# A fused attention, gated convolution, Fourier and FFN kernel: how its first pair of heads is loaded and where its early weights are decoded

## The chip, the cores and the metric

The kernel runs on one core of one Trainium2 chip. The core has TensorE for matmuls (PE in the profile; its weight loads are PEld), VectorE (DVE), ScalarE (ACT), GpSimd (POOL) and SyncE, whose queue (SPq) issues nearly all DMAs. The metric is device time of one execution in microseconds (us).

## The reference

Inputs are float32. Attention over 8 batches, 8 heads, 576 positions and 64 columns a head is followed by a gated causal convolution, a two-dimensional Fourier mixing, a layer norm and a feed-forward block:

```
scores = q @ k.T / 8            # masked: a block of 64 rows sees its own and earlier blocks
attn = softmax(scores) @ v      # heads joined: x is (8, 576, 512)
gate = sigmoid(causal_conv5(x, conv_w));  x = (gate * (x @ w_val)) @ w_out
u = x + real(fft(fft(x, axis=1), axis=2))
un = (u - mean(u)) / sqrt(var(u) + 1e-6)
out = u + relu(un @ w_ch1) @ w_ch2
```

The weights w_val, conv_w, w_out, w_ch1 and w_ch2 are float64 in memory. The kernel reads their bits and makes float32 of them.

## The kernel before

The first half of the kernel, phase1, does attention, the gated convolution and the Fourier part; the second, phase2, the norm and the feed-forward block for nine groups of 512 tokens. Every float32 operand of a matmul is split into a high and a low part in a reduced format (fp32r), and a product is two or three matmuls of parts.

**Pairs and units.** Two heads form a pair; there are 32 pairs, four to a batch. A pair is nine units: units 0 to 7 are a block of 128 queries of one of its two heads, unit 8 is the last 64 queries of both. One loop runs over the unit number n (288 units and a few to drain). A unit's stages lie apart in the loop: the scores on PE (emit_qk, L417 and L418, for unit 8 L181 to L183, tile sc), the row maximum on DVE (emit_max, L441 and L449, tile mx), the exponential on ACT (emit_exp, L463, tile PB), six units later the transposes on PE (emit_t, L577, tile pt) with copies on ACT (L583, tiles PTa, PTb, PTc), and the product with v (emit_near and emit_av, L544 and L605, tile av). The first five pairs scale by the sums of the exponentials through a transpose (L513, L524, L531).

**Operands of a pair.** `load` fetches q and k of a pair as one tile each of 128 partitions (two heads of 64), `split` writes the high and low parts (QHL and KP on ACT, the low part of q on DVE, KL on POOL), and DMAs from SBUF to SBUF copy them into the places that the matmuls read: K (L375, k with one head in both halves), QD (L364) and QQ (`spread`, L388 and L390).

**Dense work.** When the four pairs of a batch are done, `dense(b)` makes the batch's convolution gate, product with w_val (tile psv), product with the folded w_out (psx) and the Fourier products (psy, pss). It is a generator; each step emits a piece. A credit decides how many steps a unit takes: 0.9 up to unit 60 (RATE0, N0), 1.25 after (RATE).

**Early weights.** `prep_weights` is a generator too. Part by part (four of w_val, four of w_out, 128 rows of 512 each) it loads raw bits into the tile XA, decodes them (`decode`: one ACT instruction L71, four DVE instructions L75, L76, L80, L82) and writes high and low parts (wv_h L55 on DVE, wv_l L274 on POOL; for w_out the fold L295 to L299 on POOL, then we_h and we_l). Then it loads the DFT tables in ten pieces through XA and casts each to its place (L321 on ACT). It advances with the steps of the loop:

```
if pend[0] is prep:
    ...
else:
    next(pend[0])
    next(prep, None)
```

So the first parts of the weights come with the first units, and the rest comes only together with the dense steps of batch 0, which start at unit 42; what is then left is run at once ahead of that batch's product with w_out.

The tile framework turns the program into one queue of instructions for each engine. Each engine works its queue strictly in order and waits on semaphores. The framework moves instructions in the queues by its own schedule, so their order is not that of the text.

Of the kernel before, what the change touches and what calls it, by code (L numbers as in the profile page):

```python
# [8 lines left out]
F32 = mybir.dt.float32  # L9
F32R = mybir.dt.float32r  # L10
# [7 lines left out]
def kernel(  # L18
# [15 lines left out]
    D = 512  # L34
# [82 lines left out]
    def phase1():  # L117
        with ExitStack() as c1:
# [44 lines left out]
            dft_t = pool.tile([P, dft.shape[1]], F32R, name="dft")  # L163
            o = [0]

            def table(n, w):
                t = dft_t[:, o[0]:o[0] + n * w]
                o[0] += n * w
                return t.rearrange("p (n w) -> p n w", w=w) if n > 1 else t
            CDH, CDL, SDH, SDL = table(2, 258), table(2, 258), table(2, 256), table(2, 256)  # L170
            CMH, CML, SMH, SML = table(2, N2), table(2, N2), table(2, N2), table(2, N2)
            CQ, CT1, CT2, ST = table(1, 258), table(1, N2), table(1, N2), table(1, N2)
# [55 lines left out]
            YD = 2  # L228
# [6 lines left out]
            def prep_weights():  # L235
                for t in (XSP, YC2, YS2):
                    nc.gpsimd.memset(t.bitcast(F32), 0.0)
                xa = XA.rearrange("p a b c -> p (a b c)")
                raws = [(xa[:, D * 2 * i:D * 2 * i + D * 2], []) for i in range(2)]
                vals = [(t[:, 0:D], []) for t in gvs]  # L240
                uP = xa[:, 4 * D:5 * D]
                cnt = [0, 0]

                def take(pool, at):
                    t, users = pool[cnt[at] % len(pool)]
                    cnt[at] += 1
                    for c in users:
                        c.run()
                    users.clear()
                    return t, users  # L250

                def load_decode(src, n, dst, more=()):
                    raw, users = take(raws, 0)
                    r = raw.bitcast(I32)[:, 0:2 * n]
                    nc.sync.dma_start(out=r, in_=src)
                    c = Chain(wait, wait, wait, *decode(r, dst), *more)
                    users.append(c)
                    return c

                def run_all(cs):  # L260
                    for c in cs:
                        c.run()

                c0 = load_decode(conv_w.bitcast(I32), 20, uP[:, 0:20], (
                    lambda: nc.vector.tensor_copy(out=cw.rearrange("p c t -> p (c t)"), in_=uP[:, 0:20]),))
                yield
                for c in range(4):
                    d, users = take(vals, 1)

                    def w_hi(d=d, h_=wv_h[:, c, :]):  # L270
                        copy(5, h_, d)

                    def w_lo(d=d, h_=wv_h[:, c, :], l_=wv_l[:, c, :]):
                        nc.gpsimd.tensor_tensor(out=l_, in0=d, in1=h_.bitcast(F32), op=ALU.subtract)  # L274
                    users.append(load_decode(w_val[c * P:(c + 1) * P, :].bitcast(I32), D, d, (w_hi, w_lo)))
                    for _ in range(YD):
                        yield
                c0.run()
                run_all([c for _, us in raws + vals for c in us])
                for t in GF:  # L280
                    nc.gpsimd.memset(t, 0.0)

                raws[:] = [(xa[:, 0:2 * D], [])]
                vals[:] = [(xa[:, 2 * D:3 * D], [])]
                yield 1
                prev = None
                for c in range(4):
                    w, users = take(vals, 1)
                    part = load_decode(w_out[c * P:(c + 1) * P, :].bitcast(I32), D, w)
                    for _ in range(YD):  # L290
                        yield

                    def fold(w=w, part=part):
                        part.run()
# [6 lines left out]
                    def e_hi(c=c):  # L301
                        copy(6, we_h[:, c, :], uP[:, 0:D])

                    def e_lo(c=c):
                        nc.gpsimd.tensor_tensor(out=we_l[:, c, :], in0=uP[:, 0:D], in1=we_h[:, c, :].bitcast(F32),
                                                op=ALU.subtract)
                    if prev is not None:
                        prev.run()
                    prev = Chain(wait, wait, wait, wait, fold, e_hi, e_lo)
                    users.append(prev)  # L310
                    yield
                prev.run()

                w = dft.shape[1] // NCH
                chunks = []
                for z in range(NCH):
                    t = xa[:, z % 4 * w:z % 4 * w + w]
                    if z > 3:
                        chunks[z - 4].run()
                    nc.sync.dma_start(out=t, in_=dft[:, z * w:z * w + w])  # L320
                    chunks.append(Chain(wait, wait, wait, lambda t=t, z=z: (  # L321
                        nc.scalar.copy if CE >> z & 1 else nc.vector.tensor_copy)(out=dft_t[:, z * w:z * w + w], in_=t)))
                    yield
                run_all(chunks)
# [15 lines left out]
            def load_v(p):  # L340
                if p >= NPAIR:
# [4 lines left out]
                    out=VV[p], in_=v[b, :, hp * P:(hp + 1) * P].rearrange("(t p) c -> p t c", p=P))  # L346

# [301 lines left out]
            def dense(b):  # L649
# [57 lines left out]
                else:  # L707
                    for _ in prep:
                        tick(list(live))
# [205 lines left out]
            N0 = 60  # L915
            RATE0 = 0.9
# [11 lines left out]
            PS = 6  # L928
            prep = prep_weights()
            prepared = [0]  # L930
            load(0)
            nc.gpsimd.memset(PB[8][:, S:640], 0.0)
            for t in QD + [QQ[h][g][rs[1 - h], 1, :] for h in range(2) for g in range(2)]:
                nc.gpsimd.memset(t.bitcast(F32), 0.0)
            split(0).run()
            spread(0, 0)
            spread(0, 1)
            load_v(0)
            load(1)
            pend = [prep]  # L940
            next(prep)
            credit = 0.0

            def step(k=1):
                while k > 0 and pend:
                    try:
                        if pend[0] is prep:
                            if prepared[0] == PS:
                                pend.pop(0)
                                continue  # L950
# [363 lines left out]
```

## Time and profile before

| | us |
|---|---|
| median of 3 runs | 1477.8 |
| lowest and highest of them | 1476.51, 1479.29 |
| the profiled execution, its time | 1476.05 |
| the profiled execution, its span (first to last instruction) | 1474.2 |

The span is cut into stretches below by the first score matmul of a pair: pair 0 begins at 11.94 us, pair 1 at 30.39, pair 2 at 50.24, pair 3 at 70.43, pair 4 at 84.75, pair 5 at 99.89, pair 6 at 118.52, pair 7 at 143.07, pair 8 at 161.92, pair 12 at 237.09. PE's busy share is over the whole stretch; "PEclk" is the TensorE clock granted, as a share of full speed (2.4 GHz; half is 1.2 GHz).

### The profile page before, as it was taken

To read this page: it belongs to the slowest core of one execution; us is meant where nothing else is said; L and a number is where in the kernel's file an instruction comes from. 1 tells how busy PE (TensorE), PEld (TensorE's weight loads), DVE (VectorE), ACT (ScalarE), POOL (GpSimd) and SP (SyncE) were. 2 spreads that over 40 slices of the span, in tenths; PEclk is the share of its full clock that TensorE was granted. 3 is DMA by queue.
4 is the path that set the end of the run, shared out by engine and by line. 5 is a ranking of instruction groups with operands and counts; after the bars stand their busy time and mean duration, and the time that the engine had idled before them with its cause. 6 is when DMAs were issued, how large, how long until landed. Compare 5 with 4: busy or idle time off the path is not lost.

```text
span 1474.2 us, 22875 instructions
## 1 busy us (share of the span) xinstructions
PE 1420.3 (96%) x8543; PEld 1205.5 (82%) x8543; DVE 815.5 (55%) x1618; ACT 644.5 (44%) x1627; POOL 309.7 (21%) x254
## 2 busy tenths in 40 slices
PE   5798999999999999999999999999999999999998
PEld 3576888999989898888788888888888888888887
DVE  5777797979797979898983222322232223222212
ACT  5687777777777777734532112121121212112110
POOL 3423232323232323222011011111011111011100
PEclk9799999999999999999999999999999999999999
DMA  7567565656565656353500010100101010010000
GB/s 207 151 161 212 152 179 145 173 148 176 146 177 147 174 150 167 99 175 114 204 29 29 0 57 1 57 0 17 42 0 57 1 53 5 0 58 1 29 0 29
DMA packets 121611, 137.22 MB, mean 93 GB/s; under 512 B 23567, under 2 KB 91421, under 8 KB 121501
## 3 DMA queue, kind: packets, MB, share of 16 engines
q1 hardware_dynamic: 120960, 135.63, 32.2%
q8 instruction: 67, 1.10, 0.3%
q14 instruction: 44, 0.35, 0.1%
q10 hardware_dynamic: 540, 0.14, 0.0%
HBM read 70.57 MB, written 19.01 MB: 61 GB/s over the span
## 4 chain that ended last, share of the span: by engine, by line
PE 73%; DVE 10%; issue 6%; DMA 4%; POOL 3%; ACT 3%; SPq 1%; DVEq 0%; ACTq 0%; POOLq 0%
PE psh L1187 8%; PE psh L1185 8%; PE psh L1186 8%; PE o L1206 8%; PE o L1204 8%; PE o L1205 8%; PE av L605 4%; PE pt L577 4%; DVE gate L632 2%; PE sc L417 2%; POOL XA L838 2%; PE sc L418 2%; PE psx L181 1%; DVE mx L449 1%; PE psx L182 1%
## 5 line engine op out<-in xcount | busy, mean ns | idle before, releaser
L1191 DVE SCALAR_TENSOR_TENSOR hl<-psh,hh 128x512 fp32r<-128x512 f32 x144 | 99.4, 690 | 398.4 <-ACT hh L1190 398.3
L1190 ACT ACTIVATE hh<-psh 128x512 fp32r<-128x512 f32 x144 | 86.1, 598 | 500.2 <-PE psh L1187 500.0
L1187 PE MATMUL psh<-UTH,W 128*128 128x512 f32 x504 | 196.2, 389 | 1.2 <-DVE W L1093 1.2
L1185 PE MATMUL psh<-UTH,W 128*128 128x512 f32 x504 | 196.2, 389 | 1.1 <-ACT W L1092 1.1
L1206 PE MATMUL o<-hl,W 128*128 128x512 f32 x504 | 196.2, 390 | 0.0
L1186 PE MATMUL psh<-UTL,W 128*128 128x512 f32 x504 | 196.1, 389 | 0.0
L1204 PE MATMUL o<-hh,W 128*128 128x512 f32 x504 | 196.1, 389 | 0.0
L1205 PE MATMUL o<-hh,W 128*128 128x512 f32 x504 | 196.0, 389 | 0.0
L463 ACT ACTIVATE PB<-sc,mx 128x128 f32<-128x128 f32 (+4 forms) x320 | 167.0, 527 | 52.8 <-DVE mx L449 29.5
L577 PE MATMUL pt<-ident,PB 128*128 128x128 f32 x800 | 141.9, 283 | 15.4 <-ACT PTb L583 8.1
L577 PEld LDWEIGHTS pt<-ident,PB 128*128 128x128 f32 x800 | 101.0, 144 | 32.5 <-ACT PTb L583 14.5
L632 DVE SCALAR_TENSOR_TENSOR gate<-XF,cw,gate 128x575 f32<-128x575 f32 (+3 forms) x128 | 122.2, 955 | 4.5 <-ACT gate L63 3.6
L1187 PEld LDWEIGHTS psh<-UTH,W 128*128 128x128 f32 x504 | 94.6, 188 | 21.3 <-DVE W L1093 1.6
L1215 POOL TENSOR_TENSOR U<-o,U 128x512 f32<-128x512 f32 x32 | 40.3, 1288 | 341.0 <-DVE o L1213 341.0
L1185 PEld LDWEIGHTS psh<-UTH,W 128*128 128x128 f32 x504 | 94.6, 188 | 21.1 <-ACT W L1092 1.5
L1206 PEld LDWEIGHTS o<-hl,W 128*128 128x128 f32 x504 | 94.5, 188 | 20.6 <-DVE hl L1191 1.0
L1204 PEld LDWEIGHTS o<-hh,W 128*128 128x128 f32 x504 | 94.6, 188 | 19.9 <-ACT hh L1190 0.2
L1205 PEld LDWEIGHTS o<-hh,W 128*128 128x128 f32 x504 | 94.6, 188 | 19.8
L1186 PEld LDWEIGHTS psh<-UTL,W 128*128 128x128 f32 x504 | 94.6, 188 | 19.6
L449 DVE TENSOR_REDUCE mx<-sc 128x1 f32<-128x384 f32 (+2 forms) x192 | 104.3, 560 | 4.4 <-PE sc L183 2.7
L417 PE MATMUL sc<-K,QQ 128*128 128x256 f32 (+2 forms) x256 | 87.9, 354 | 13.4 <-DMA QQ<-QHL 12.5
L628 POOL TENSOR_TENSOR XL<-XF,XH 128x576 fp32r<-128x576 f32 x32 | 45.9, 1434 | 249.3 <-ACT XH L57 249.1
(226 smaller groups left out, 3122.0 us busy)
## 6 DMA issues: line engine op xcount, KB each, us to landing
K<-KP SPq DMA_DIRECT2D x128, 144.0 KB, 2.5
QQ<-QHL SPq DMA_DIRECT2D x128, 128.0 KB, 2.5
rw<-in_w_ch SPq DMA_DIRECT2D x28, 512.0 KB, 7.2
VV<-in_v SPq DMA_DIRECT2D x32, 320.0 KB, 3.6
qraw<-in_q SPq DMA_DIRECT2D x32, 288.0 KB, 3.3
kraw<-in_k SPq DMA_DIRECT2D x32, 288.0 KB, 3.3
out<-U SPq DMA_DIRECT2D x36, 256.0 KB, 2.0
QQ<-QHL SPq DMA_DIRECT2D x128, 64.0 KB, 2.4
```

Source lines behind the costliest of these rows:

```text
L417: nc.tensor.matmul(t[:, o:o + w], q[:, 0, m], KK[p][h][:, 0:w], start=True, stop=False)
L449: nc.vector.reduce_max(out=mx[:, j:j + 1], in_=t, axis=AX.X, negate=one)
L463: nc.scalar.activation(out=PB[i][:, k0:k0 + w], in_=t, func=AF.Exp, bias=nm, accum_out=su[:, at + j:at + j + 1])
L577: nc.tensor.transpose(ps[:, j, :], PB[i][:, (j0 + j) * P:(j0 + j + 1) * P], ident)
L632: nc.vector.scalar_tensor_tensor(out=gate[c][:, s:S], in0=XF[:, 0:S - s], scalar=cw[:, c, 4 - s:5 - s], in1=gate[c][:, s:S], op0=ALU.mult, ...
L1185: nc.tensor.matmul(ps, W1H[f][:, c * P:c * P + P], UTH[g][:, c, :], start=(c == 0), stop=False)
L1186: nc.tensor.matmul(ps, W1H[f][:, c * P:c * P + P], UTL[g][:, c, :], start=False, stop=False)
L1187: nc.tensor.matmul(ps, W1L[f][:, c * P:c * P + P], UTH[g][:, c, :], start=False, stop=(c == 3))
L1191: nc.vector.scalar_tensor_tensor(out=l, in0=ps, scalar=0.0, in1=h.bitcast(F32), op0=ALU.max, op1=ALU.subtract)
L1204: nc.tensor.matmul(po[t], W2H[e][:, c], h, start=(e == 0), stop=False)
L1205: nc.tensor.matmul(po[t], W2L[e][:, c], h, start=False, stop=False)
L1206: nc.tensor.matmul(po[t], W2H[e][:, c], l, start=False, stop=(e == NF - 1))
```

## The change

Three things are changed.

1. **First pair.** `first_pair` takes the place of `load(0)`, `split(0)` and both `spread(0, .)`. q and k of pair 0 are loaded twice each, head by head into both halves of the partitions, in two column halves: 16 DMAs of 64 partitions, eight issued from SyncE and eight from ScalarE. They land in tiles that are free at that time (gate). ACT and DVE then write QQ, K, KL, KP and QD in place, and the 14 DMAs from SBUF to SBUF of pair 0 are gone. Its parts are emitted in the loop at units 1, 2 and 4.
2. **Early weights.** The raw bits have four places of their own in the space of the DFT tables (tile stage), which are made only after the last decode. Loads, decodes and table pieces have fixed units (VU, OU, TU) instead of coming with the steps: w_val at units 0 to 9, w_out at 13 to 25, tables at 32 to 44.
3. **Dense steps.** The credit is 1.25 from the start.

```diff
+            VU = (0, 3, 6, 9)
+            OU = (13, 17, 21, 25)
+            TU = (32, 32, 33, 33, 34, 38, 38, 39, 39, 40)
...
+                slots = [stage[:, 2 * D * i:2 * D * i + 2 * D] for i in range(4)]
...
+                load_conv()
+                load_part(w_val, 0)
+                for c in range(1, 4):
+                    at_unit(c - 1, load_part, w_val, c)
+                at_unit(0, do_conv)
+                for c in range(4):
+                    at_unit(VU[c], do_val, c)
+                    at_unit(VU[c] + 6, load_part, w_out, c)
+                    at_unit(OU[c], do_out, c)
                 for z in range(NCH):
...
+                    at_unit(TU[z], load_table, z)
+                    at_unit(TU[z] + 4, do_table, z)
...
+            def first_pair():
+
+                *KK[0], KP[0], KL[0] = k_places()
+                Q0, K0, T0 = gate[0:2], gate[2:4], XFS
+                halves = slice(0, 256), slice(256, S)
+                dma = [nc.sync.dma_start, nc.scalar.dma_start]
+                for c in halves:
+                    for x, to in ((q, Q0), (k, K0)):
+                        for h in range(2):
+                            for r in rs:
+                                dma[h](out=to[h][r, c], in_=x[0, 0][rs[h], c])
...
+                def q_part(g):
+                    c = slice(256 * g, 256 * g + 256)
+                    for h in range(2):
+                        a, z = rs[h], rs[1 - h]
+                        nc.scalar.activation(out=T0[h][z, c].bitcast(F32R), in_=Q0[h][z, c], func=AF.Copy, scale=0.125)
+                        nc.scalar.activation(out=QQ[h][g][a], in_=Q0[h][a, c].unsqueeze(1).to_broadcast([64, 2, 256]),
+                                             func=AF.Copy, scale=0.125)
+                        nc.vector.scalar_tensor_tensor(out=QQ[h][g][z, 0, :], in0=Q0[h][z, c], scalar=0.125,
+                                                       in1=T0[h][z, c], op0=ALU.mult, op1=ALU.subtract)
+
+                def k_part(c):
+                    for h in range(2):
+                        nc.vector.tensor_copy(out=KK[0][h][:, c], in_=K0[h][:, c])
+                    for h in range(2):
+                        a = rs[h]
+                        nc.vector.tensor_tensor(out=KL[0][a, c], in0=K0[h][a, c], in1=KK[0][h][a, c].bitcast(F32),
+                                                op=ALU.subtract)
...
+                q_part(0)
+                k_part(halves[0])
+                return lambda: k_part(halves[1]), lambda: q_part(1), last_part
...
-            N0 = 60
-            RATE0 = 0.9
             RATE = 1.25
...
-            load(0)
...
-            split(0).run()
-            spread(0, 0)
-            spread(0, 1)
...
-                            next(pend[0])
-                            next(prep, None)
+                        next(pend[0])
...
-                credit += RATE if n > N0 else RATE0
+                prep_at(n)
+                credit += RATE
```

The queues show what moves. The first place is the start of ACT's queue. Before, it holds (after the load of the activation table) the high parts of q and k of pair 0, a decode and the first exponential:

```order
L356 ACT_TABLE_LOAD
L356 ACTIVATE QHL<-qraw 128x576 [waits DMAHW0_49]
L57 CAST KP<-kraw 128x576 [waits DMAHW1_49]
L71 ACTIVATE XA<-XA 128x20 [waits DMAHW3_49]
L71 ACTIVATE gv_153<-XA 128x512 [waits DMAHW4_49]
L463 ACTIVATE PB_121,su<-sc,mx 128x128 [waits DVE_49,PE_49]
```

In the changed kernel it begins with eight DMA issues; DMAHW0 to DMAHW7 are the semaphores of DMAs, which all DMAs of the core take in turn:

```order
L366 DMA gate_150<-in_q 64x256 x2
L366 DMA gate_152<-in_k 64x256 x2
L366 DMA gate_150<-in_q 64x320 [waits DMAHW0_49]
L366 DMA gate_150<-in_q 64x320 [waits DMAHW2_49]
L366 DMA gate_152<-in_k 64x320 [waits DMAHW4_49]
L366 DMA gate_152<-in_k 64x320 [waits DMAHW6_49]
L374 ACT_TABLE_LOAD
L374 ACTIVATE XF_134<-gate_149 64x256 [waits DMAHW3_49]
L375 ACTIVATE QQ_117<-gate_149 64x512 [waits DMAHW1_49]
L374 ACTIVATE XF_135<-gate_150 64x256
L375 ACTIVATE QQ_119<-gate_150 64x512
L374 ACTIVATE XF_134<-gate_149 64x256 [waits DMAHW3_49]
```

The last four of the eight issues stand behind waits on the first loads, and the table load and all of ACT's work stand behind these.

The second place is PE's queue at the change from pair 0 to pair 1. Before, the transposes of units 5 to 8 of pair 0 (PB_126 to PB_129) stand ahead of the first scores of pair 1 (K_227):

```order
L524 MATMUL rt<-ident,XF_134 128x128 x2
L544 MATMUL av<-PTa_130,VV 64x256
L544 MATMUL av<-PTa_130,VV 64x128 x2
L577 MATMUL pt<-ident,PB_126 128x128 x3
L577 MATMUL pt<-ident,PB_127 128x128 x4
L577 MATMUL pt<-ident,PB_128 128x128 x4
L577 MATMUL pt<-ident,PB_129 128x128 x5
L544 MATMUL av<-PTb,VV 64x320
L417 MATMUL sc<-K_227,QQ_117 128x256
```

In the changed kernel the eight score matmuls of pair 1 (K_238, K_239) stand ahead of them:

```order
L190 MATMUL sc<-KP,QD_115 128x320
L190 MATMUL sc<-KP,QD_115 128x256
L596 MATMUL av<-PTa_130,VV 64x128
L469 MATMUL sc<-K_238,QQ_117 128x256
L470 MATMUL sc<-KL,QQ_117 128x256
L469 MATMUL sc<-K_238,QQ_117 128x256
L470 MATMUL sc<-KL,QQ_117 128x256
L469 MATMUL sc<-K_239,QQ_119 128x256
L470 MATMUL sc<-KL,QQ_119 128x256
L469 MATMUL sc<-K_239,QQ_119 128x256
L470 MATMUL sc<-KL,QQ_119 128x256
L576 MATMUL rt<-ident,XF_134 128x128 x2
```

The third place is DVE's queue in the middle of pair 0. Before, the maxima of the later units (L449) come first and one decode follows (w_val's second part, gv_154):

```order
L359 SCALAR_TENSOR_TENSOR QHL<-qraw,QHL 128x576
L447 MEMSET sc 64x64
L505 RECIPROCAL re<-su 128x2x2
L449 TENSOR_REDUCE mx<-sc 128x1 x3
L75 TENSOR_SCALAR gv_154<-gv_154 128x512
L451 TENSOR_REDUCE mx<-mx 128x1
L76 TENSOR_SCALAR gv_154<-gv_154 128x512
```

In the changed kernel two decodes, w_val's first and second part, stand ahead of the maxima of units 5 and 6 (the last row):

```order
L80 SCALAR_TENSOR_TENSOR XA<-stage,XA 128x512
L76 TENSOR_SCALAR XA<-XA 128x512
L82 SCALAR_TENSOR_TENSOR XA<-stage,XA 128x512
L80 SCALAR_TENSOR_TENSOR XA<-stage,XA 128x512
L276 CAST wv_h<-XA 128x512
L82 SCALAR_TENSOR_TENSOR XA<-stage,XA 128x512
L394 SCALAR_TENSOR_TENSOR QD_115<-gate_149,QD_115 64x64
L394 SCALAR_TENSOR_TENSOR QD_115<-gate_150,QD_115 64x64
L276 CAST wv_h<-XA 128x512
L499 MEMSET sc 64x64 x2
L501 TENSOR_REDUCE mx<-sc 128x1 x2
```

The decodes have moved ahead of scores that wait for their maxima.

## Rows read from the trace of the kernel before

**Rows 1.** The page: the span, and each engine's busy time and share.

```profile
span 1474.2 us, 22875 instructions
PE 1420.3 (96%) x8543; PEld 1205.5 (82%) x8543; DVE 815.5 (55%) x1618; ACT 644.5 (44%) x1627; POOL 309.7 (21%) x254
```

**Rows 2.** Stretches cut at pairs: length, busy of PE, PEld, DVE, ACT, POOL; clock; DMA.

```profile
0.00:11.94 11.94, 0.00 (x0) 0.00 (x1) 5.13 (x10) 3.52 (x5) 5.12 (x18) 1.00 0.75 203
11.94:30.39 18.45, 15.37 (x60) 10.53 (x60) 9.48 (x31) 11.00 (x34) 5.17 (x6) 0.81 0.76 209
30.39:50.24 19.85, 14.53 (x76) 10.47 (x76) 15.99 (x35) 11.63 (x32) 6.16 (x5) 0.77 0.59 154
50.24:70.43 20.19, 14.82 (x83) 10.26 (x82) 16.75 (x36) 13.96 (x41) 11.07 (x14) 0.84 0.54 146
70.43:84.75 14.32, 13.08 (x89) 9.83 (x88) 9.62 (x29) 11.95 (x36) 3.53 (x4) 0.95 0.54 140
84.75:99.89 15.14, 15.08 (x100) 10.35 (x99) 9.32 (x28) 12.39 (x37) 4.18 (x4) 1.00 0.72 188
99.89:118.52 18.63, 17.13 (x130) 15.02 (x128) 16.02 (x45) 14.26 (x40) 6.82 (x8) 1.00 0.71 191
118.52:143.07 24.55, 20.17 (x147) 15.81 (x146) 18.15 (x44) 19.18 (x53) 5.80 (x6) 0.93 0.72 211
143.07:161.92 18.85, 17.89 (x146) 15.71 (x144) 13.13 (x30) 15.16 (x45) 6.92 (x7) 1.00 0.57 136
161.92:237.09 75.17, 73.13 (x627) 65.60 (x625) 62.01 (x140) 56.01 (x161) 23.31 (x17) 1.00 0.64 175
```

**Rows 3.** The timeline of all engines, first 15 us: start, length, engine, line, operation, wait.

```profile
0.73 1.28 ACT L356 ACT_TABLE_LOAD   x1 [0.73 <-PEq L1301]
...
0.74 0.39 SPq L336 DMA_DIRECT2D qraw<-in_q  x1
...
3.61 0.69 ACT L356 ACTIVATE QHL<-qraw 128x576 fp32r<-128x576 f32 x1 [1.59 <-DMA qraw<-in_q]
...
4.32 0.76 DVE L359 SCALAR_TENSOR_TENSOR QHL<-qraw,QHL 128x576 fp32r<-128x576 f32 x1 [4.32 <-ACT QHL L356]
...
5.22 2.83 SPq L375 DMA_DIRECT2D K<-KP  x4
...
11.94 0.58 PE L417 MATMUL sc<-K,QQ 128*128 128x256 f32 x1 [11.94 <-DMA QQ<-QHL]
...
13.99 0.42 DVE L441 TENSOR_REDUCE mx<-sc 128x2 f32<-128x256 f32 x1
```

**Rows 4.** The chain of waits, 95 to 146 us: start, length, what.

```profile
98.74 8.00 DMA XA<-in_w_out
...
139.21 3.01 DMA XA<-in_dft
```

**Rows 5.** DVE's timeline in pair 0.

```profile
11.98 0.43 DVE L55 CAST wv_h<-gv 128x512 fp32r<-128x512 f32 x1
...
26.11 0.42 DVE L549 TENSOR_TENSOR XF<-av,XF 128x256 f32<-128x256 f32 x1 [2.20 <-PE av L544]
```

**Rows 6.** DVE's timeline in pair 1: first, last instruction of a decode, its cast.

```profile
33.03 0.43 DVE L75 TENSOR_SCALAR gv<-gv 128x512 f32<-128x512 f32 x1 [0.27 <-ACT gv L71]
...
34.68 0.69 DVE L82 SCALAR_TENSOR_TENSOR gv<-XA,gv 128x512 int32<-128x512 int32 x1
...
35.40 1.51 DVE L55 CAST wv_h<-gv 128x512 fp32r<-128x512 f32 x1
```

**Rows 7.** Waits from 11.94 to 84.75 us: who for whom, total, times, longest.

```profile
DVE sc L440 <- PE sc L418: 9.8, 5, 4.7
```

**Rows 8.** PE's timeline: two neighbouring matmuls of dense work at full clock.

```profile
82.29 0.29 PE L182 MATMUL psv<-XL,wv_h 128*128 128x288 f32 x1
82.42 0.29 PE L183 MATMUL psv<-XH,wv_l 128*128 128x288 f32 x1
```

**Rows 9.** POOL's timeline in pair 1, beside that cast.

```profile
34.89 1.74 POOL L370 TENSOR_TENSOR KL<-kraw,KP 128x576 fp32r<-128x576 f32 x1 [8.60 <-ACT KP L57]
```

More of the change, by code (lines that the diff above doesn't have):

```diff
@@ L233, in phase1, with prepare @@
             CE = 1023
-            def prep_weights():
+            def prepare():
                 for t in (XSP, YC2, YS2):
                     nc.gpsimd.memset(t.bitcast(F32), 0.0)
[L238 to L279, printed above, removed]
@@ L280, in prep_weights @@
                 for t in GF:
                     nc.gpsimd.memset(t, 0.0)
[L283 to L294, printed above, removed]
+                xa = XA.rearrange("p a b c -> p (a b c)")
@@ new lines, in prepare, with ordered @@
+                slots = [stage[:, 2 * D * i:2 * D * i + 2 * D] for i in range(4)]
+                small = stage[:, 8 * D:8 * D + 40]
+                vals = [xa[:, D * i:D * i + D] for i in range(2)]
+                uPs = [xa[:, 2 * D + D * i:2 * D + D * i + D] for i in range(2)]
+                taps = xa[:, 4 * D:4 * D + 20]
+                order = []
+                def ordered(*stages):
+                    c = Chain(*stages)
+                    order.append(c)
+                    return c
@@ L324, in prep_weights, with load_table @@
-                run_all(chunks)
+                    ordered(*decode(slots[c], w), fold, wait, wait, wait, lambda: nc.scalar.copy(out=h_, in_=uP), wait,
+                            lambda: nc.gpsimd.tensor_tensor(out=l_, in0=uP, in1=h_.bitcast(F32), op=ALU.subtract))
+                NS_, CW = 5, dft.shape[1] // NCH
+                def load_table(z):
+                    if z == 0:
+                        for o in order:
+                            o.run()
+                        make_tables()
+                    nc.sync.dma_start(out=xa[:, z % NS_ * CW:z % NS_ * CW + CW], in_=dft[:, z * CW:z * CW + CW])
@@ new lines, in do_table, with at_unit @@
+                def do_table(z):
+                    to, t = tables["dft"][:, z * CW:z * CW + CW], xa[:, z % NS_ * CW:z % NS_ * CW + CW]
+                    ordered(lambda: (nc.scalar.copy if CE >> z & 1 else nc.vector.tensor_copy)(out=to, in_=t))
+                todo = {}
+                def at_unit(n, f, *a):
+                    todo.setdefault(n, []).append((f, a))
+                load_conv()
+                load_part(w_val, 0)
+                for c in range(1, 4):
+                    at_unit(c - 1, load_part, w_val, c)
@@ L327, in phase1 @@
+                return at, rest
             NPAIR = B * NP
@@ L707, in dense @@
                 else:
-                    for _ in prep:
-                        tick(list(live))
+                    prep_rest()
+                CDH, CDL, SDH, SDL, CMH, CML, SMH, SML, CQ, CT1, CT2, ST = (
+                    tables[t] for t in "CDH CDL SDH SDL CMH CML SMH SML CQ CT1 CT2 ST".split())
                 xt = ((2, 1), (3, 1), (0, 0), (1, 0), (2, 0), (0, 1), (1, 1), (3, 0))
@@ L976, in phase1 @@
                     emit_qk(n)
+                    if n in (1, 2, 4):
+                        later[(1, 2, 4).index(n)]()
                     if i in (4, 8):
```

99 lines of the change are left out of this document (54 added, 45 removed).

## The prediction

> **What bounds the kernel now.** I read the page first: PE is busy for 96% of a span of 1474.2 us [rows 1], so a change that adds and removes no matmul can only win back time that PE loses. Where it loses is read from the table of stretches, cut at the pairs of heads [rows 2]. From pair 8 to pair 12 PE is busy 73.13 of 75.17 us at full clock: there the kernel is bound by PE. Before pair 8 it is not. Pairs 0 to 3 take 18.45, 19.85, 20.19 and 14.32 us although they hold almost no dense work, and the granted clock is 0.81, 0.77, 0.84 and 0.95 (a mix of the levels 1.2 and 2.4 GHz) in stretches where PE waits. Ahead of them lie 11.94 us without a matmul. Pair 6 takes 24.55 us, more than any later one. The timeline of the first 15 us [rows 3] shows why PE starts late: q is issued at 0.74 us, ACT has it at 3.61, four copies of k take SyncE 2.83 us, more copies follow in that queue, and the first score waits until 11.94. DVE takes its first maximum at 13.99. In the chain of waits around pairs 5 to 7 [rows 4] a load of w_out takes 8.00 us and a table piece 3.01 us: the early weights are late for batch 0's dense work.
>
> After pair 27 the queues of both programs hold the same dense columns at each pair, and the total is the same (592,762, counted over the order). So the end moves by what PE loses less before pair 8, and by nothing else. I sum in three parts.
>
> **The start.** The first loads go out at 0.74 us as before. An issue took 0.39 us and data were there 2.87 us after it (0.74 to 3.61) [rows 3], so the fourth load of each queue is issued at about 1.9 us and lands at 4.8. ACT's eighth issue waits for that and ends near 5.2; the table load of 1.28 us [rows 3], which ran beside the loads before, now follows it, to 6.5. Four ACT instructions for the first half at 0.4 to 0.65 us (from 0.69 for 576 columns [rows 3]) end at 8.6, so the first score comes at 7.6 to 8 instead of 11.94. But the first maximum gains less. ACT's queue has pair 1's q and k ahead of pair 0's first exponential, and SyncE issues their loads only behind its own eight and v: they land near 10.5. DVE has the second halves and pair 1's low part of q ahead of its first maximum. I put it at 12.5, a gain of 1.5. If a load of 64 partitions costs as much to issue as a copy of k (2.83 / 4 = 0.71 us [rows 3]), all comes 1 us later.
>
> The Trainium skill speaks against this part: "SBUF — State Buffer", section "Can I just issue two DMAs to hit both halves?", says that DMAs on two halves of the partitions serialize and that several issuing engines do not help. By that rule the second loading of the same bytes costs what it saves, and the start gains nothing; this is the first rival below.
>
> **DVE from there to pair 4.** Pair 4's first score is at 84.75 us. Up to there DVE was busy 5.13 + 9.48 + 15.99 + 16.75 + 9.62 = 56.97 us and idle 27.78 [rows 2]; 8.3 us of that idle time lie before the first maximum (13.99 less 5.13 and some 0.6 of work after 11.94 [rows 2, 3, 5]), 19.5 behind it: 7.5 in pair 0 and 3.86 + 3.44 + 4.70 = 12.0 in pairs 1 to 3.
>
> - A decode takes 33.03 to 35.37, 2.35 us [rows 6]. Six of the eight lay before pair 4 and now all eight do: + 4.7.
> - Pair 0's split is now 14 DVE instructions: 4 casts at 0.26 (half of 0.43 for 512 columns [rows 5], with some fixed cost), 8 subtractions at 0.44 (0.42 for 256 columns [rows 5]), two small ones at 0.15. That is 4.9, less the 0.76 of the old low part of q [rows 3]: + 4.1.
>
> This gives 65.8 us of work, and 7.3 us idle before the first maximum (12.5 less some 5.2 of work). What is open is the idle time behind it. If none is left, pair 4's first score comes at 73.1 (- 11.7); if all 19.5 stay, at 92.6 (+ 7.9). In pair 0 the queue of DVE now holds three and a half decodes, so nearly all of the 7.5 goes. In pairs 0 to 3 DVE waited 9.8 us for scores of PE at the first maximum of a pair [rows 7], and pair 1's scores now stand ahead of sixteen transposes; but two decodes ahead of the maxima of units 5 and 6 hold up their exponentials. I take 8.0 us, nearer to pairs 1 to 3 alone (12.0) than to nothing: 65.8 + 7.3 + 8.0 = 81.1, or **- 3.7 us**. POOL and SyncE do the same kinds of work as before here; SyncE has 14 copies fewer.
>
> **Pairs 4 to 7.** Counted over the order, pairs 8 to 11 hold 73,344 dense columns and take 75.17 us [rows 2]. A dense matmul of 288 columns takes 0.13 us from start to start [rows 8]. Pairs 4 to 7 held 50,866 columns, 22,478 fewer, or 78 matmuls, 10.1 us: at PE's pace 65.1 us. They took 77.17 (15.14 + 18.63 + 24.55 + 18.85 [rows 2]), so 12.1 were lost, and of these 9.1 in pair 6 (10,992 columns: 15.5 at PE's pace against 24.55). Now two decodes, their folds and the wait for the loads are gone from pairs 5 to 7; the ten table casts move from pairs 6 and 7 to 4 and 5, beside ACT's 12.39 of 15.14 us there. I leave 5 us of loss (0 to 12.1). With RATE 1.25 the four pairs hold 56,928 columns, so 75.17 - 7.4 + 5 = 72.8: **- 4.4 us**. The 6,062 columns more that are then done (21 matmuls, 2.7 us) and 576 more ahead of pair 4 (0.3) need not be done later: **- 3.0 us**.
>
> **The sum** is - 3.7 - 4.4 - 3.0 = - 11.1 us on the profiled execution's 1476.05: 1465.0. The median of the runs shown lies 1.75 above that execution, so I say 1466.5 for a median.
>
> **A cost that the order hides.** A cast of 512 columns took 0.43 us, and 1.51 us where a subtraction of POOL ran beside it from 34.89 to 36.63 [rows 5, 6, 9]. The Trainium skill's page "SBUF — State Buffer", section "Who interferes with whom", says that such an operation and GpSimd lock each other out of a shared port; the trace agrees with 1.51 against 0.43. The 56.97 us include such losses for the POOL work of six parts; the two folds that now also fall before pair 4 bring six more long POOL instructions. At 1.08 us each that is 6.5 at most and 0 at least; I took 0, since pair 4's queue has room for the last of them, and the second rival takes all.
>
> **Rivals.**
>
> 1. *The double load brings nothing* (0.12). The 16 loads land when the copies did, and the first maximum stays at 13.99. For it: DMA share 0.75 in the first stretch [rows 2] and the waits in ACT's queue. Against it: 14 copies leave. It costs the 1.5 us of the start: 1466.5, median 1468.
> 2. *The early decodes hold up the pairs* (0.12, slower). DVE waits as before (+ 7.9) and POOL's six instructions each lengthen one of DVE's by 1.08 us (+ 6.5). That is + 14.4 at pair 4 and + 7.0 with the rest: 1483.1, median 1485. For it: DVE was already busy 16 of 20 us in pairs 1 and 2. Against it: it was idle half of pair 0. It decides when pair 4's first score comes later than 84.75 + 7.4 = 92.2 us.
> 3. *The parts cancel* (0.10). DVE's idle time stays at 19.5 but POOL costs nothing: + 7.9 - 7.4 = + 0.5, median 1478.
> 4. *The early pairs flow* (0.14). DVE hardly waits any more, PE keeps its clock, and pairs 4 to 7 lose 2 us: - 11.7 - 7.4 - 3.0 = - 22.1, median 1456. For it: no single engine has more than about 17 us of work in a pair of 20.
>
> **How the numbers follow.** The forecast itself has 0.52, with a range of its own from 1459 to 1473 (idle time 4 to 12, loss 2 to 8). This kernel's runs tell some 0.2% (3 us) from no change. The forecast, rivals 1 and 4 are faster (0.77, less a small tail), rival 3 is about the same (0.11 with that tail), rival 2 is slower (0.12). The range from 1453 to 1478 leaves out rival 2, part of 3 and the far end of 4.
>
> **What would show it.** Right: the first score at 7.5 to 9 us and the first maximum near 12.5; DVE's busy share above 0.85 in pair 0; pair 4's first score at 77 to 85; pair 6 under 19 us; 70 to 76 us from pair 4 to pair 8; from pair 12 on a constant lead. Wrong: a first score of pair 4 later than 88 us, long DVE instructions beside POOL's folds in pairs 1 to 3, exponentials that wait for maxima behind decodes, a lead that changes after pair 12, or a wait of SyncE for the last decodes ahead of the tables that delays the copies of pair 5.

## The result, and the profile of the changed kernel

| | before | changed |
|---|---|---|
| median, us | 1477.7 (4 runs) | 1496.7 (4 runs) |
| lowest and highest, us | 1476.51, 1479.29 | 1494.84, 1501.53 |
| profiled execution, us | 1476.05 | 1495.39 |

The ratio is 1.0133, with a 95% interval from 1.0106 to 1.016. The change makes the kernel slower by 19 us; 1466.5 was forecast, with a range from 1453 to 1478.

The page of the changed kernel answers to [rows 1]: the same matmuls, and yet both PE and DVE are busy longer (DVE 836.0 us against 815.5).

```profile
span 1493.6 us, 22873 instructions
PE 1427.8 (96%) x8543; PEld 1208.0 (81%) x8543; DVE 836.0 (56%) x1631; ACT 650.5 (44%) x1637; POOL 316.2 (21%) x253
```

Stretches cut at the pairs say where the time goes; columns as in [rows 2]. First the start and pairs 0 to 4 (pairs 2 and 3 left out), then the batches of pairs 8 to 11 and 16 to 19, and last pairs 12 to 27 as one stretch:

```profile
0.00:10.61 10.61, 0.00 (x0) 0.03 (x1) 2.13 (x7) 4.19 (x7) 4.25 (x18) 1.00 0.70 195
10.61:24.39 13.78, 11.74 (x40) 7.76 (x40) 13.53 (x35) 10.29 (x30) 4.74 (x3) 1.00 0.95 295
24.39:48.45 24.06, 16.77 (x94) 12.30 (x93) 22.71 (x54) 17.21 (x50) 12.74 (x14) 0.83 0.67 177
...
83.88:107.94 24.06, 17.99 (x105) 12.04 (x103) 13.54 (x40) 18.53 (x50) 3.61 (x4) 0.93 0.90 262
...
160.55:239.12 78.57, 74.05 (x633) 66.92 (x632) 64.78 (x146) 56.27 (x163) 21.98 (x17) 1.00 0.58 152
...
318.45:397.72 79.27, 75.06 (x634) 66.50 (x633) 63.68 (x145) 55.73 (x163) 23.17 (x17) 1.00 0.57 151
...
239.12:552.91 313.79, 299.15 (x2527) 267.29 (x2525) 254.99 (x578) 225.11 (x653) 94.85 (x65) 1.00 0.58 152
```

And the two like stretches of the kernel before, which the prediction had not asked for: pairs 16 to 19, and pairs 12 to 27.

```profile
312.25:386.53 74.28, 73.28 (x640) 67.16 (x638) 60.36 (x145) 56.19 (x166) 22.35 (x16) 1.00 0.60 161
...
237.09:535.13 298.04, 293.66 (x2550) 268.56 (x2549) 242.59 (x579) 224.87 (x658) 89.05 (x64) 1.00 0.60 160
```

The reader is to see two things. Up to pair 8 the changed kernel is ahead: pair 4 begins at 83.88 us (84.75 before), pair 8 at 160.55 (161.92 before), with 6,638 more dense columns done (counted over the order, as in the prediction). Then, at full clock, every batch of four pairs is slower: 79.27 against 74.28 us. Pairs 12 to 27 take 15.75 us more (313.79 against 298.04), and DVE is busy 12.40 us more in them, for the same work. PE is idle for 10.26 us of the 15.75 (14.64 against 4.38). Behind pair 28 another 1.6 us are lost (940.7 us to the end against 939.1).

### The profile page after: what moved, and what is told of

Its sections match the earlier page's. It is cut to its first block, busy times and chain, and to the rows that moved or that the text cites. A ratio compares the mean times of both kernels' runs of the same rounds, so it can differ in the third digit from the quotient of the medians.

```text
span 1493.6 us, 22873 instructions
## 1 busy us (share of the span) xinstructions
PE 1427.8 (96%) x8543; PEld 1208.0 (81%) x8543; DVE 836.0 (56%) x1631; ACT 650.5 (44%) x1637; POOL 316.2 (21%) x253
## 4 chain that ended last, share of the span: by engine, by line
PE 69%; DVE 13%; DMA 6%; ACT 5%; issue 3%; SPq 2%; POOL 2%; ACTq 0%; DVEq 0%; POOLq 0%
PE psh L1224 8%; PE psh L1222 8%; PE o L1243 8%; PE psh L1223 8%; PE o L1241 8%; PE o L1242 8%; PE av L657 3%; DVE gate L684 3%; PE pt L629 3%; ACT PB L515 2%; DVE mx L501 1%; PE sc L469 1%; PE sc L470 1%; DMA QQ<-QHL 1%; PE psv L188 1%
## 5 line engine op out<-in xcount | busy, mean ns | idle before, releaser
L684 DVE SCALAR_TENSOR_TENSOR gate<-XF,cw,gate 128x575 f32<-128x575 f32 (+3 forms) x128 | 132.1, 1032 | 2.0 <-ACT gate L63 1.7
```

The costliest lines, as they stand in the source:

```text
L684: nc.vector.scalar_tensor_tensor(out=gate[c][:, s:S], in0=XF[:, 0:S - s], scalar=cw[:, c, 4 - s:5 - s], in1=gate[c][:, s:S], op0=ALU.mult, ...
```

## The experiments

**Which part of the change.** My theory, A: the third part did it, since the new credit moves the dense steps against the units. Theory B: the first two parts, by the order of the DMA queues and the places of the tiles. The first run undoes part three alone, the second makes it alone:

```diff
-                credit += RATE
+                credit += RATE if n > 60 else 0.9
```

> The changed kernel with the old credit again (0.9 up to unit 60, then 1.25); parts 1 and 2 of the change stay. Theory A (the rate sets where in a batch the dense steps fall, and that costs the steady batches 4 to 5 us each): pairs 12 to 16, 16 to 20 and 20 to 24 take 74 to 75.5 us each as in the kernel before, and the time is 1473 to 1479 us, since at pair 8 the changed kernel had only a small lead. Theory B (parts 1 and 2, by the order of the DMA queues and the places of the tiles, cost the steady batches): the batches stay at 78.5 to 79.5 us and the time at 1492 to 1499.

Measured: 1474.8 us, ratio 0.9976 [0.9963, 0.9988]; pairs 16 to 19 take 74.24 us, pairs 12 to 27 298.23:

```profile
232.65:530.88 298.23, 293.61 (x2550) 268.75 (x2549) 242.71 (x579) 223.92 (x658) 88.99 (x64) 1.00 0.60 160
```

```diff
-            N0 = 60
+            N0 = -1
```

> The kernel before with the credit at 1.25 from the start, nothing else. Theory A: batches of 78 to 80 us from pair 12 on, time 1492 to 1500. Theory B: batches of 74 to 75.5 us, time 1472 to 1480.

Measured: 1510.9 us, ratio 1.0219 [1.0202, 1.0236]; pairs 12 to 27 take 313.63 us. Theory A holds and B falls. The third part costs the steady batches all they lose, and the time lies above A's range because pair 8 begins already at 176.35 us, 14.4 later than before; in that kernel the early weights come with the steps too, which may be why.

**What of the new credit.** From unit 60 on the old and the new credit differ in two ways: dense work runs some six steps earlier, and the unit that takes two steps is another one of four. Each is undone alone, then both:

```diff
-            credit = 0.0
+            credit = 0.5
```

> The changed kernel with the credit starting at 0.5 instead of 0. A unit takes two dense steps when the credit passes a whole number twice, once in four units; with 36 units in a batch these units are always the same: n = 3, 7, 11, ... in the changed kernel, n = 1, 5, 9, ... in the kernel before and in this one. The dense steps done up to any unit stay the same within one. Theory A1 (it is the place of the double steps in the four units): batches of 74 to 75.5 us, time 1473 to 1480. Theory A2 (it is that dense work runs some six steps earlier in each batch): batches of 78 to 80, time 1492 to 1500; the same by theory B.

Measured: 1495.4 us, ratio 1.0115 [1.0099, 1.013]; pairs 12 to 27 take 315.84 us.

```diff
                 credit -= nst
+                if 42 <= n < 47:
+                    nst = 0
```

> The changed kernel with the steps of units 42 to 46 left out, so that dense work runs six steps later against the units, as in the kernel before (40 steps up to unit 78 instead of 46), while the double steps stay at n = 3, 7, 11, ... Theory A2 (earlier dense work costs it): batches of 74 to 75.5 us, time 1473 to 1480. Theory A1 (the place of the double steps): batches of 78 to 80, time 1492 to 1500; the same by theory B.

Measured: 1495.5 us, ratio 1.0116 [1.0101, 1.0131]; pairs 12 to 27 take 308.73 us, so a third of what these pairs lose is back; but from pair 28 to the end this kernel takes 945.0 us, where the changed kernel takes 940.7. Neither A1 nor A2 alone: both missed.

> The changed kernel with both edits of the two kernels before: the steps of units 42 to 46 left out and the credit starting at 0.5. From unit 60 on each dense step then falls at the same unit as with the old credit (17 steps at unit 60, 40 at 78, 62 at 96, double steps at n = 1, 5, 9, ...). Theory A3 (lag and place of the double steps only work together: what counts is the order of the queues as a whole): batches of 74 to 75.5 us from pair 8 on, time 1472 to 1479. If something in the first 42 units made the batches slow (theory B in another form), they stay at 77 to 80 and the time at 1493 to 1500.

Measured: 1476.1 us, ratio 0.9984 [0.9971, 0.9996]; pairs 12 to 27 take 298.98 us. Only the two together give the old batches back. There is no better or worse rate here; one order of the queues fits and three near it don't.

**What makes an order fit.** The group of the gate taps on DVE (L684; `tap` in the text, a product and a sum of two operands that lie in SBUF) gave the lead. First pairs 12 to 27 of the changed kernel, columns as on the page:

```profile
L684 DVE SCALAR_TENSOR_TENSOR gate<-XF,cw,gate 128x573 f32<-128x573 f32 (+1 forms) x65 | 71.9, 1106 | 0.8 <-ACT gate L63 0.8
```

and the same group in the kernel before:

```profile
L632 DVE SCALAR_TENSOR_TENSOR gate<-XF,cw,gate 128x574 f32<-128x574 f32 (+1 forms) x65 | 61.9, 953 | 0.6
```

The timeline of the changed kernel in pair 17 shows a long tap and what follows from it:

```profile
338.54 3.36 POOL L891 TENSOR_TENSOR XA<-XA 128x580 f32<-128x580 f32 x2 [2.71 <-DVE XA L915]
...
339.11 1.49 DVE L684 SCALAR_TENSOR_TENSOR gate<-XF,cw,gate 128x575 f32<-128x575 f32 x1
...
340.77 1.75 DVE L684 SCALAR_TENSOR_TENSOR gate<-XF,cw,gate 128x574 f32<-128x574 f32 x1
...
341.86 1.93 POOL L422 TENSOR_TENSOR KL<-kraw,KP 128x576 fp32r<-128x576 f32 x1
...
342.44 0.41 DVE L493 TENSOR_REDUCE mx<-sc 128x2 f32<-128x256 f32 x1
...
343.14 0.67 DVE L523 TENSOR_TENSOR su<-su 128x2 f32<-128x2 f32 x1
...
343.74 0.80 DVE L684 SCALAR_TENSOR_TENSOR gate<-XF,cw,gate 128x573 f32<-128x573 f32 x1
...
345.21 0.20 DVE L528 RECIPROCAL re<-su 128x10 f32<-128x10 f32 x1
345.46 0.09 PEld L538 LDWEIGHTS rt<-ident,re 128*10 128x10 f32 x1 [1.38 <-DVE re L528]
345.46 0.28 PE L538 MATMUL rt<-ident,re 128*10 128x128 f32 x1 [1.14 <-DVE re L528]
```

Two taps beside POOL's additions take 1.49 and 1.75 us; a third, with POOL idle, takes 0.80. A sum of two columns ends with POOL's subtraction for the low part of k and takes 0.67. So DVE comes late to the reciprocal, and PE stands 1.14 us for it. Over pairs 12 to 27 PE's waits for this reciprocal (total, times, longest) are, in the changed kernel and in the kernel before:

```profile
PE rt L538 <- DVE re L528: 8.7, 10, 1.6
...
PE rt L486 <- DVE re L476: 2.0, 7, 0.4
```

In pairs 16 to 19 ten of 17 taps run over 1 us, each beside a POOL instruction; with the old credit four of 17. Theory C: the new order lays DVE's instructions beside POOL's, DVE falls behind, and PE waits for it. Rival D: the order costs it whatever POOL does. The next two kernels take POOL's long instructions out of the steady part under either order (the low part of k is left out, with a copy of k on ACT in its place, and the other results are left out but for 8 columns):

```diff
-                    nc.gpsimd.tensor_tensor(out=kl, in0=kraw[p], in1=kh.bitcast(F32), op=ALU.subtract)
+                    if p < 8:
+                        nc.gpsimd.tensor_tensor(out=kl, in0=kraw[p], in1=kh.bitcast(F32), op=ALU.subtract)
+                    else:
+                        nc.scalar.copy(out=kl, in_=kraw[p])
...
+                    w = slice(0, S if p < 8 else 8)
+                    nc.gpsimd.tensor_tensor(out=xl[:, w], in0=XF[:, w], in1=xh[:, w].bitcast(F32), op=ALU.subtract)
...
```

> The changed kernel with the long instructions of POOL in the steady part taken away: from pair 8 on the low part of k is a copy on ACT instead of a subtraction on POOL, and from batch 2 on POOL's other subtractions and additions (low part of x, of the Fourier inputs, the last butterflies) do 8 columns instead of 288 to 576 (these results are left out). In the changed kernel 10 of 17 gate taps of a batch ran longer than 1 us, each beside a POOL instruction, against 4 of 17 with the old credit, and the mean tap was 1.21 us against 0.94. Theory C (the new order puts taps beside POOL's work, DVE falls behind and PE waits for it): taps of 0.7 to 0.8 us, batches from pair 12 on of 73.5 to 75.5 us, time 1475 to 1482. Theory D (the order of the queues costs the time also where POOL is out of the way): batches of 77.5 to 79.5, time 1490 to 1498.

Measured: 1461.7 us, ratio 0.9888 [0.9876, 0.9901]; pairs 12 to 27 take 297.13 us, the mean tap 0.81 us.

> The control for the run above: the changed kernel with the old credit, and the same POOL instructions shortened or replaced. By both theories batches of 73 to 75 us and 1468 to 1475. What decides is the gap between the two kernels: without the shortening it was 20 us; theory C says at most 7, theory D 14 or more.

Measured: 1458.2 us, ratio 0.9859 [0.9846, 0.9871]; pairs 12 to 27 take 291.83 us, the mean tap 0.79 us. The two stretches, new order and old:

```profile
234.87:532.00 297.13, 294.02 (x2526) 267.22 (x2525) 225.85 (x578) 232.62 (x671) 21.57 (x48) 1.00 0.61 161
...
235.67:527.50 291.83, 291.34 (x2551) 269.04 (x2549) 224.06 (x577) 231.23 (x674) 17.78 (x48) 1.00 0.61 164
```

Both times lie below their expectations; both kernels also take some 10 us less behind pair 28 (929 us), which had not been counted. The gap between the orders falls from 21.9 us (1496.7 against 1474.8) to 3.5 us, as C says, and PE's wait for the reciprocal is gone in both. Over pairs 12 to 27 the gap falls from 15.56 (313.79 less 298.23) to 5.30: two thirds went with POOL's long instructions. What is left need not all be the order's own. In pairs 12 to 15 both kernels still run four long additions of POOL, those of batch 1, and in the new order alone two taps beside them take over 1 us (1.27 and 1.38); in pairs 16 to 27 the gap falls from 11.65 to 2.63. DVE's instructions also stand in a somewhat other order in each of these two kernels than in the kernel that it was made from. So the shares are rough, and D is right for a third at most.

**Late results or slow neighbours.** Shorter POOL instructions also give their results earlier. So in one kernel ACT writes a copy of k where the low part belongs (the low part is left out), and POOL does its old subtraction all the same, into the raw k, which nobody reads any more; in the other POOL's subtraction is gone. The queues of PE, DVE and ACT are the same in both.

```diff
...
+                        nc.scalar.copy(out=kl, in_=kraw[p])
+                        nc.gpsimd.tensor_tensor(out=kraw[p], in0=kraw[p], in1=kh.bitcast(F32), op=ALU.subtract)
```

> The changed kernel; from pair 8 on the low part of k is a copy on ACT (the subtraction is left out), and POOL does its old subtraction all the same, into the raw k that nobody reads any more. So the result comes early, but POOL is as long beside VectorE as before. Theory C1 (VectorE's instructions run longer beside POOL's, and that makes VectorE late): taps of 1.1 to 1.25 us, batches of 77.5 to 79.5, time 1490 to 1500. Theory C2 (POOL's results came late): as the next kernel within 3 us.

Measured: 1496.6 us, ratio 1.0119 [1.0103, 1.0135]; pairs 12 to 27 take 315.34 us, DVE busy 254.17.

> The same without POOL's subtraction, so that 7 of the 14 overlaps of taps with POOL's instructions in a batch are gone. Theory C1: taps of 0.9 to 1.05 us, batches of 75 to 77.2, time 1478 to 1487, and 8 us or more faster than the kernel above. Theory C2: no difference to the kernel above.

Measured: 1481.3 us, ratio 1.0013 [1.0002, 1.0024]; pairs 12 to 27 take 305.31 us, DVE busy 241.92. The taps measured 1.04 us (a little less than expected) and 0.93. The two stretches, with POOL's subtraction and without it:

```profile
238.61:553.95 315.34, 299.18 (x2526) 268.51 (x2525) 254.17 (x576) 233.45 (x670) 94.48 (x65) 0.99 0.58 152
...
237.13:542.44 305.31, 295.55 (x2526) 267.27 (x2525) 241.92 (x576) 232.03 (x670) 67.82 (x48) 1.00 0.60 156
```

Instructions whose results nobody uses, one in each pair from pair 8 on, cost 15.25 us of the median. The same place in the two timelines, pair 19; first with POOL's subtraction:

```profile
376.96 1.43 POOL L426 TENSOR_TENSOR kraw<-kraw,KP 128x576 f32<-128x576 f32 x1 [1.22 <-ACT KL L425]
377.01 1.99 DVE L688 SCALAR_TENSOR_TENSOR gate<-XF,cw,gate 128x574 f32<-128x574 f32 x1
...
379.54 0.80 POOL L791 TENSOR_TENSOR XOOL<-XA,XOOH 128x290 fp32r<-128x290 f32 x1 [1.15 <-DVE XOOH L788]
379.71 1.24 DVE L688 SCALAR_TENSOR_TENSOR gate<-XF,cw,gate 128x573 f32<-128x573 f32 x1
```

and without it:

```profile
371.70 0.69 ACT L425 CAST KL<-kraw 128x576 fp32r<-128x576 f32 x1
...
372.52 0.80 DVE L687 SCALAR_TENSOR_TENSOR gate<-XF,cw,gate 128x574 f32<-128x574 f32 x1
...
373.86 0.82 POOL L790 TENSOR_TENSOR XOOL<-XA,XOOH 128x290 fp32r<-128x290 f32 x1 [2.61 <-DVE XOOH L787]
374.03 1.25 DVE L687 SCALAR_TENSOR_TENSOR gate<-XF,cw,gate 128x573 f32<-128x573 f32 x1
```

The tap that ran beside POOL's subtraction falls from 1.99 to 0.80 us; the one beside the low part of the Fourier input stays at 1.25. C1 is shown for this instruction, C2 falls. POOL's subtraction also frees the raw k later for its next load, but that is not the cause: ACT waits for such a load twice in this stretch, 1.3 us in all.

Two more readings of the traces bear on this. First, take the median of each kind of DVE instruction where no POOL instruction overlaps it: over pairs 12 to 27 those that do overlap one ran some 34 us longer than that in the changed kernel, some 20 in the kernel before and in the first run (an estimate from the traces). The difference is about DVE's additional 12.40 us. Second, without POOL's subtraction DVE is no busier than in the kernel before (241.92 against 242.59 us), and yet these pairs take 7.27 us more. So not all of the loss shows in DVE's busy time.

**Is it one wait?** The wait at the transpose of the reciprocals is the largest single one, so it was given one unit more:

```diff
-                if n >= FR and PN <= pr < NPAIR and ir == 1:
+                if n >= FR and PN <= pr < NPAIR and ir == 2:
```

> The changed kernel with PE's transpose of the reciprocals (tile rt) one unit later in the loop. In the steady batches of the changed kernel PE stood 1.8 us a batch at this transpose for the reciprocal of DVE, the largest single wait of the 5 us that a batch lost. If a wait at one place is what costs: batches of 76.5 to 77.5, time 1486 to 1491. If DVE's lateness only shows next at another place (the scaling of the output of v, the row maxima): batches as before, 1493 to 1500.

Measured: 1505.2 us, ratio 1.0181 [1.0168, 1.0194]; pairs 12 to 27 take 321.18 us. Worse than both: DVE stays as busy (256.38 us). In pairs 16 to 19 PE's wait for the reciprocals is gone, but it waits 2.4 us for ACT's copies of the transposes and 2.0 for ACT's exponentials (0.5 and 1.3 in the changed kernel); as I read it, what hangs on the transpose of the reciprocals now starts later. Mending where a late engine shows does not make it less late.

**The first two parts, and the tables.** These runs measure the terms of the prediction. Part one alone on the kernel before, and part two alone (the kernel of the first run with the old start):

> The kernel before with the first part of the change alone (q and k of pair 0 loaded twice and split in place). As predicted: the first maximum comes some 1.5 us earlier, and that is kept to the end: 1475 to 1477.3. Rival: what is gained at the first score is lost in pair 0, since DVE has 4 us more to do there, or waits of pairs 5 to 7 for the early weights take it: 1477.5 to 1480.

Measured: 1480.3 us, ratio 1.0003 [0.9992, 1.0014]. The first score comes at 9.62 us, pair 4 at 80.26 (4.5 us earlier than before), but pair 8 at 163.02: pairs 4 and 5 take 18.0 and 21.9 us, where the kernel before took 15.1 and 18.6, and pair 6 still takes 23.8. All is given back there. By the time the rival holds, at the edge of its range. Of its reasons the second holds in part: in pairs 5 and 6 the chain of waits runs through decodes of w_out on DVE and folds on POOL; pair 4 it did not name.

> The changed kernel with the old credit and the old first pair, so with the second part of the change alone (early weights staged in the place of the tables). If the second part brings what the two parts bring together: pair 8 at 157 to 159 and 1473 to 1476. If the first part brings it: 1476 to 1480 and pair 8 at 160 to 163.

Measured: 1479.5 us, ratio 1.0000 [0.9988, 1.0012], pair 8 at 165.25. Pairs 5 to 7 flow, but pair 0 takes 22.8 us with the early decodes in it, and pair 4, with the table casts, 26.6. Neither part gains alone; together (the first run) they bring pair 8 to 157.61 and the end 3 us forward. As I read it, part two takes away the late weights that cost part one its lead, and part one the long pair 0 that costs part two; no run shows that step by step.

> The changed kernel with the old credit, and with the ten table pieces loaded at units 32, 34, ... 50 and cast four units later, instead of all between units 32 and 44. Pair 4 took 23.77 us with ten casts of some 0.6 us on ACT in it and a DMA share of 0.91, the other pairs around it 14.5 to 16. If the casts and their loads are what pair 4 waits for: pairs 4 and 5 together take 33 to 36 us instead of 38.27, pair 8 begins at 153 to 156, the time is 1467 to 1472. If it is the other work of the batch's change (gate taps, pair 5's operands): pair 4 stays above 22 us and the time at 1472 to 1477.

Measured: 1473.3 us, ratio 0.9957 [0.9943, 0.9972]. Pair 4 takes 20.7 us, pairs 4 and 5 37.8, pair 8 begins at 157.31, hardly earlier than in the first run (157.61): between the two expectations, with the time in the range of the second. Pair 5, which was free of casts, now takes its share of them.

> The changed kernel with the old credit, and with the decodes of w_out at units 15, 21, 27 and 33 instead of 13 to 25 and the table pieces at units 36, 38, ... 54 (casts up to unit 58; the dense work of batch 0 first wants them at unit 61). DVE was busy 21.8 of 23.15 us in pair 1. If DVE's decodes set the length of pairs 1 and 2: pairs 0 to 3 together take 70 to 73 us instead of 74.8, pair 8 begins at 152 to 156 and the time is 1466 to 1471. If the pairs are set by something else (PE's slower clock, the sums of the first five pairs): 74 to 76 us and 1472 to 1477, as with the tables alone spread.

Measured: 1471.1 us, ratio 0.9957 [0.9944, 0.997]. Pairs 0 to 3 take 75.0 us, not less, so DVE's decodes do not set them. But pair 4 takes 17.2 us and pair 8 begins at 154.29: the gain lies in pairs 4 to 7 (69.5 us, 73.5 in the first run). The tables still later are the likely cause; w_out's decodes moved in the same run and are not told apart from them.

**The subtraction on DVE.** If POOL's 1.7 us cost DVE more than the 0.7 us that DVE would need itself, it belongs on DVE:

```diff
-                    nc.gpsimd.tensor_tensor(out=kl, in0=kraw[p], in1=kh.bitcast(F32), op=ALU.subtract)
+                    nc.vector.tensor_tensor(out=kl, in0=kraw[p], in1=kh.bitcast(F32), op=ALU.subtract)
```

> The changed kernel with the low part of k as a subtraction on VectorE. Theory C1: the overlaps of the taps with it go, VectorE gets 3 us more of its own: batches of 75.5 to 77.5, time 1481 to 1490. If VectorE's total is what counts, not the overlaps: 1495 to 1505.

Measured: 1486.0 us, ratio 1.0050 [1.0032, 1.0068]; pairs 12 to 27 take 304.02 us, DVE busy 251.38. DVE does 16 subtractions more and is busy 3.6 us less than in the changed kernel.

> The kernel with the old credit, w_out's decodes at units 15 to 33 and the tables at 36 to 54, and with the low part of k as a subtraction on VectorE (some 0.75 us) instead of POOL (1.65 us). VectorE takes 3 us more a batch and loses the overlaps with these four instructions. If the overlaps were worth about that: batches of 74 to 74.8 and 1468 to 1472. If VectorE's place in the queue counts more (the subtraction ahead of row maxima): 1473 to 1482.

Measured: 1468.9 us, ratio 0.9929 [0.9916, 0.9943]: the fastest of the kernels that leave nothing out, and faster than both kernels of the comparison. It gains in the early pairs (pair 8 at 151.39); its steady pairs 12 to 27, 299.62 us, are no shorter than in the first run (298.23). In this order, whose taps had met POOL less often, the move gains nothing there.

## Why the prediction was wrong

**The step that failed** is "the end moves by what PE loses less before pair 8, and by nothing else", and with it "from pair 12 on a constant lead". I had counted the dense columns at each pair and found them equal after pair 27, and took equal work for equal time. But the third part shifts the dense steps against the units in every batch, and DVE's and POOL's instructions with them. By batches from pair 8 on that cost 3.40, 4.17, 4.99, 4.18 and 2.41 us, 19.15 in all, against a lead of 1.37 at pair 8; at pair 28 the kernel is 17.78 us behind. The prediction had named a lead that changes after pair 12 among the signs of being wrong, and that is what came. The experiments show the cause: the order alone (first five runs). Some two thirds of the loss go when POOL's long instructions go, and for one of these, the low part of k, the way is shown: DVE's instructions run longer beside it, and PE waits for them. The rest, at most 1.3 us a batch, has no single place that I could show and stays open.

The price had stood in the prediction, as "a cost that the order hides": 1.08 us for a cast beside POOL [rows 5, 6, 9]. It was asked only of the pairs before pair 4, where code had moved, and not of the steady batches, where the same code runs in another order. Before pair 4 the 0 that I took was nearly right: by the same estimate as above, such stretches came to some 8 us there, and to some 7 in the kernel before. The Trainium skill's page "SBUF — State Buffer", section "Who interferes with whom", has the rule that tells which instructions to look for: one of VectorE with two inputs in SBUF excludes one of GpSimd that reads SBUF, one with at most one such input does not, unless it runs in one of the two-port modes, which a cast can enter. The trace agrees: a tap, with both inputs in SBUF, took 1.99 us beside POOL's subtraction and 0.80 without it, and the row maximum at 342.44 in pair 17, which reads scores of PE, took 0.41 us beside the subtraction for the low part of k.

**The start** was mis-sized. Two issues took 1.12 to 1.48 us, so one took 0.56 to 0.74 and not 0.39, near the prediction's own "if" of 0.71. The table load began at 6.33 us, after the eighth issue, where 5.2 was said. The first score came at 10.61, not 7.6 to 8. The timeline of the changed kernel shows what it waited for:

```profile
9.68 0.33 DVE L382 CAST K<-gate 128x320 fp32r<-128x320 f32 x1 [2.86 <-DMA gate<-in_k]
...
10.04 0.42 DVE L377 SCALAR_TENSOR_TENSOR QQ<-gate,XF 64x256 fp32r<-64x256 f32 x1
...
10.61 0.77 PE L469 MATMUL sc<-K,QQ 128*128 128x256 f32 x2 [10.61 <-ACT QQ L375]
```

DVE's cast of a second half of k waits for its load and stands ahead of the low part of q, which ends at 10.46; the score follows 0.15 us later. The profile names an instruction of ACT as the releaser, but in the first run and in three other kernels with this start the first score also comes 0.14 to 0.15 us after the low part of q, and ahead of the end of that instruction of ACT. Over all the other kernels with this start it came at 9.13 to 10.03. The prediction had put the second halves ahead of the first maximum, not of the first score. The first maximum came at 14.68, later than before (13.99), not at 12.5: ahead of it a subtraction of 0.41 us took 1.46 beside POOL's first subtraction. With part one alone it came at 13.21, which is half of the gain of 1.5 that was said. So the first rival was not far off for the changed kernel, but that the start gains nothing is not what part one alone shows (first score 2.3 us earlier, pair 4 4.5 us). Whether the DMAs of the two halves serialize, no run here shows.

**DVE up to pair 4.** The work was 64.15 us (65.8 forecast), the idle time 19.7 (15.3 forecast), so pair 4 came at 83.88 and not 81.1. The ledger was good, the idle terms too small: 8.6 us before the first maximum (7.3 forecast) and 11.2 behind it (8.0).

**Pairs 4 to 7** took 76.67 us instead of 72.8: the loss that I put at 5 us was 8.9. Pair 6 lost its wait as forecast (16.68 us from 123.54), but the ten table casts moved into pair 4, which took 24.06: ACT 18.53 us busy, DMA share 0.90. Only "beside ACT's 12.39 of 15.14 us" had stood for that. Later tables, in the run that also moved w_out's decodes, took up to 6.6 us from pair 4.

**The rivals.** The slower side came in, by a mechanism that was none of the four. The second rival's condition, pair 4 after 92.2, was far from met.

## What to carry to other kernels

When a change moves one stream of work against another, compare the instructions that run side by side in a steady stretch, not only the amount of work at each mark: here equal columns hid 2.4 to 5 us a batch. Look first at the busy time of the engines that don't set the pace; the same instructions for more busy time (DVE 254.99 against 242.59) is a sign of neighbours that slow each other, though here it did not show the whole loss. An instruction that was put on an idle engine is not free if it stretches its neighbour by more than it would cost there.

## What the runs showed of the hardware

I had not expected how much one idle-looking engine can cost: 24 of POOL's subtractions of 128 by 576, from pair 8 to the end, with a result that nobody reads, cost 15.25 us, or 0.64 us each; in pairs 12 to 27 sixteen or so of them lengthened DVE's busy time by 12.25 us, 0.77 us each, though POOL is busy only a fifth of the span. And it is not the long instructions alone: a sum of two columns, 0.14 us elsewhere, took 0.67 beside POOL.
